# Where the sums of the exponentials come from: ScalarE's accumulator in one batch, a column of ones in three

## The chip, the cores and the metric

The kernel runs on one core of a Trainium2 chip. A core has TensorE (PE, matrix products), VectorE (DVE), ScalarE (ACT), GpSimd (POOL) and SyncE (SP, which here only issues DMAs); they run side by side and wait for each other by semaphores. The metric is the device time of the core in microseconds, the median of several executions.

## What is computed

Four batches of 12800 rows of 128 floats go through two attention steps against 32 inducing points, then through a gated product with a short causal convolution in the gate:

```python
def mab(q, kv):
    s = scale * (q @ kv.transpose(0, 2, 1))
    s = s - s.max(-1, keepdims=True)
    a = np.exp(s)
    a /= a.sum(-1, keepdims=True) + 1e-09
    return a @ kv
h = mab(I, x)                       # I: 32 inducing points, x: (4, 12800, 128)
x = mab(x, h)
...
for k in range(5):
    gate_pre += conv_w[k][None, None, :] * xp[:, k:k + S, :]
gate = 1.0 / (1.0 + np.exp(-gate_pre))
val = x @ w_val
return gate * val @ w_out
```

## The kernel before

**Tiling.** The 12800 rows of a batch are four strips of 3200, and a batch is cut into seven chunks of 320 to 480 columns per strip (`SIZES`). Each chunk of x comes twice: transposed, with channels on the partitions (`xt`, always a DMA), and with rows on the partitions (`xk`). For all chunks of batch 0 but one, `xk` is made on the chip by transposes on PE (`tp`, L289) and copies out of PSUM (`tpev`, L295 on ACT or L297 on DVE); for the others it is a second DMA (L258).

**The first attention of a batch.** `s1` (L315) multiplies a chunk by the inducing points, `e1` (L320, DVE) scales it into `ss` and takes the maximum; a group of chunks gets one maximum (`gm`, L337, `ng`, L365 and L367, on POOL or DVE), and then every chunk an exponential on ACT (`x1`, L375), a 32x32 transpose on DVE (`tr`, L379) and the product with `xk` on PE (`h`, L393). The products are summed in `H` (`ha`, L405 to L409). A later group has another maximum, so that what was summed before is scaled by `f` (L345).

**The sums of the exponentials.** They come from ACT: L375 has `accum_out`, which leaves the sum over a chunk's columns in a column of `zc`. Each such instruction is followed in the trace by an ACTIVATION_READ_ACCUMULATOR. When a new group comes, POOL scales the earlier columns of `zc` by `f` (`zs`, L355); at the end DVE adds the columns to `zt` (L360), PE brings `zt` into the layout of the result (`hz`, L428), and DVE takes the reciprocal (`zz`, L436 and L437). In parallel PE brings `H` into that layout (`hh`, L428), and DVE multiplies the two (`hT`, L440). `hT` is the 32x128 result h, transposed.

**What hangs on hT.** The weights of the later products (`w2`, `W`, `wo`) are derived from it (L447 to L541), and the second attention starts from it: `s2` (L555), `tin`, `mx` on DVE, `sub` (L574, POOL), `ex` (L580, ACT), `sm` (L586 to L591, DVE), `nm` (L597, POOL), `tout` (L600, DVE), and the halves of the probabilities in 16 bits, `phi` (L603, ACT) and `plo` (L605, POOL).

**The gated product.** `visit` (L622 gates, L629 values) is the convolution and the value product of a chunk on PE; `th` (L720, ACT), `gv` (L730, DVE), `hi` (L737, ACT) and `lo` (L740, POOL) make its 16-bit halves; `o` (L811, PE) is the last product, `ev` (L823 on DVE, L825 on ACT) the copy out of PSUM, `st` (L829) the store. The very last half chunk has its own path (L766 to L782).

**Order.** Nothing is scheduled at run time or by a planner: `ORDER` lists the operations one by one, each engine gets its own in this order, `SLOTS` gives every tile its buffer and `ENGINES` the engine where two can do an operation. Each engine works through its list in order, so an instruction that waits holds up all behind it. Loads of all kinds and the stores share one queue on SP.

## Time and profile before

| | us |
|---|---|
| median of 3 runs | 268.63 (267.71 to 269.29) |
| the profiled execution | 267.8 |
| its span, first to last instruction | 266.0 |
| PE busy | 260.3 (98%) |
| DVE busy | 220.4 (83%) |
| POOL busy | 202.4 (76%) |
| ACT busy | 192.4 (72%) |

The span lies 1.8 us below the time of the same execution; the rest is outside of what the instructions cover. The engines' busy times add up to far more than the span because they overlap. A PE that is busy throughout is not a PE at its peak: its matmuls overlap each other in the record. Mean time per instruction, what ended the idle time of an engine, and the chain of work that ended last say more than the shares.

### The profile page before, as it was taken

The numbers are of one execution on the slowest core, as the hardware profiler recorded it, in microseconds if no ns is written. First come the engines' busy times: TensorE is split into PE (matmuls) and PEld (weight loads), VectorE is DVE, ScalarE is ACT, GpSimd is POOL, SyncE is SP. The second block draws the span as 40 slices with busy tenths as digits, with TensorE's granted clock in tenths as the row PEclk, the third lists the DMA queues.
The fourth block names the chain that finished last, engine by engine and source line by source line (L and its number), as shares of the span: only waits on it lengthen the run. The fifth ranks groups of instructions, "written<-read, shape, count | busy, mean of one in ns | idle before, by whom it ended". The sixth has DMA issues, their size and how long they took to land.

```text
span 266.0 us, 10388 instructions
## 1 busy us (share of the span) xinstructions
PE 260.3 (98%) x4480; PEld 143.1 (54%) x4480; DVE 220.4 (83%) x438; ACT 192.4 (72%) x266; POOL 202.4 (76%) x182
## 2 busy tenths in 40 slices
PE   8999989999999999999999999999999999999994
PEld 4668343764544446584454456567545554444442
DVE  0789999997989999876998999896899897875534
ACT  2168249699759688687868599876689788787862
POOL 1013367999969878699897959999989989889660
PEclk9999999999999999999999999999999999999999
DMA  7999999699986699979998799884350324254476
GB/s 255 429 412 417 418 417 386 211 394 400 385 313 277 223 307 340 392 269 333 329 328 327 280 328 327 305 282 181 117 209 4 140 94 187 113 191 167 151 284 246
DMA packets 23229, 74.28 MB, mean 279 GB/s; under 512 B 1936, under 2 KB 16272, under 8 KB 23184
## 3 DMA queue, kind: packets, MB, share of 16 engines
q1 hardware_dynamic: 22896, 73.43, 73.5%
q8 instruction: 35, 0.57, 0.9%
q10 hardware_dynamic: 288, 0.20, 0.2%
q14 instruction: 10, 0.08, 0.1%
HBM read 47.40 MB, written 26.21 MB: 277 GB/s over the span
## 4 chain that ended last, share of the span: by engine, by line
PE 90%; DVE 8%; ACT 1%; issue 1%; POOL 0%; DVEq 0%; POOLq 0%
PE banks L622 33%; PE banks L811 24%; PE banks L555 7%; PE banks L393 7%; PE banks L315 7%; PE banks L629 6%; PE banks L289 2%; DVE et L379 2%; PE banks L216 1%; DVE ss L320 1%; PE banks L766 1%; PE banks L506 1%; DVE ng L367 1%; DVE e L559 0%; DVE z L586 0%
## 5 line engine op out<-in xcount | busy, mean ns | idle before, releaser
L740 POOL TENSOR_TENSOR gl<-tg,gh 128x960 f16<-128x960 f32 (+2 forms) x54 | 104.3, 1945 | 10.4 <-PE banks L811 5.2
L622 PE MATMUL banks<-P,W 32*128 32x480 f16 (+3 forms) x1680 | 103.9, 351 | 0.7 <-ACT P L603 0.7
L730 DVE SCALAR_TENSOR_TENSOR tg<-tg,banks 128x960 f32<-128x960 f32 (+4 forms) x57 | 61.2, 1078 | 21.7 <-ACT tg L720 14.1
L622 PEld LDWEIGHTS <-W 32*128 32x128 f16 x1680 | 51.4, 92 | 45.7 <-issue 14.9
L720 ACT ACTIVATE tg<-banks,gsc 128x960 f32<-128x960 f32 (+4 forms) x57 | 54.9, 1005 | 20.2 <-PE banks L622 18.1
L811 PE MATMUL banks<-gh,wo 128*32 128x448 f16 (+5 forms) x558 | 63.5, 358 | 0.0
L737 ACT CAST gh<-tg 128x960 f16<-128x960 f32 (+2 forms) x54 | 51.3, 961 | 11.0 <-DVE tg L730 8.7
L811 PEld LDWEIGHTS <-wo 128*32 128x32 f16 (+1 forms) x837 | 36.4, 97 | 32.8 <-issue 11.0
L811 PE MATMUL banks<-gl,wo 128*32 128x448 f16 (+4 forms) x279 | 43.5, 357 | 0.0
L629 PE MATMUL banks<-P,W 32*128 32x480 f16 (+3 forms) x336 | 41.3, 353 | 0.0
L825 ACT ACTIVATE os<-banks,osc 128x960 f32<-128x960 f32 (+2 forms) x30 | 30.5, 1024 | 6.3 <-PE banks L811 6.0
L597 POOL TENSOR_TENSOR e<-e,z 128x960 f32<-128x960 f32 (+4 forms) x17 | 24.9, 1467 | 6.2 <-DVE z L589 2.9
L393 PE MATMUL banks<-xk,et 128*32 128x128 f32 x800 | 29.5, 274 | 0.0
L823 DVE TENSOR_SCALAR os<-banks,osc 128x960 f32<-128x960 f32 (+1 forms) x24 | 27.9, 1168 | 1.4 <-PE banks L811 1.4
L605 POOL TENSOR_TENSOR P<-pt,P 128x960 f16<-128x960 f32 (+4 forms) x17 | 27.8, 1637 | 1.2 <-ACT P L603 0.9
L393 PEld LDWEIGHTS banks<-xk,et 128*32 128x32 f32 x800 | 24.8, 110 | 5.3 <-issue 1.5
L574 POOL TENSOR_TENSOR e<-e,m 128x960 f32<-128x960 f32 (+4 forms) x17 | 24.9, 1465 | 2.4 <-DVE m L569 2.4
L315 PE MATMUL banks<-xt,indT 128*32 128x480 f32 (+2 forms) x208 | 25.1, 556 | 0.0
L555 PE MATMUL banks<-xt,hT 128*32 128x480 f32 (+2 forms) x208 | 24.7, 557 | 0.0
L603 ACT CAST P<-pt 128x960 f16<-128x960 f32 (+4 forms) x17 | 14.0, 825 | 9.0 <-DVE pt L600 6.2
L559 DVE STREAM_TRANSPOSE e<-banks 128x480 f32<-128x480 f32 (+2 forms) x28 | 18.1, 652 | 1.7 <-PE banks L555 1.4
L375 ACT ACTIVATE ss<-ss,ng 128x480 f32<-128x480 f32 (+3 forms) x28 | 18.6, 665 | 0.6 <-POOL ng L367 0.6
(107 smaller groups left out, 269.8 us busy)
## 6 DMA issues: line engine op xcount, KB each, us to landing
out_dram<-os SPq DMA_DIRECT2D x30, 480.0 KB, 4.4
xt<-in_xt_dram SPq DMA_DIRECT2D x14, 960.0 KB, 8.9
xk<-in_xk_dram SPq DMA_DIRECT2D x11, 896.0 KB, 9.7
out_dram<-os SPq DMA_DIRECT2D x22, 448.0 KB, 4.5
xk<-in_xk_dram SPq DMA_DIRECT2D x10, 960.0 KB, 8.7
xt<-in_xt_dram SPq DMA_DIRECT2D x8, 896.0 KB, 11.0
xt<-in_xt_dram SPq DMA_DIRECT2D x3, 512.0 KB, 5.2
xt<-in_xt_dram SPq DMA_DIRECT2D x3, 448.0 KB, 5.9
```

The lines of the kernel that those rows point to most:

```text
L315: T.matmul(buf(key)[32 * r:32 * r + 32, :n], c_["indT"], x[:, :, r, :], start=True, stop=True)
L393: T.matmul(buf(key)[32 * s:32 * s + 32, :P], buf(("et", b, c))[:, 32 * i:32 * i + 32], buf(("xk", b, c))[:, i, :], start=j < R, stop=j >= ...
L555: T.matmul(buf(key)[32 * r:32 * r + 32, :n], buf(("hT", b)), x[:, :, r, :], start=True, stop=True)
L622: T.matmul(buf(("ps2", "g", b, c, r // 2))[:, r % 2, :n], buf(("W", b))[q, w, k, :], c_[("P1", "P2")[e]][q, o:o + n], start=u == 0, stop=u ...
L629: T.matmul(buf(("ps2", "v", b, c, r // 2))[:, r % 2, :n], buf(("W", b))[q, w, TAPS, :], c_[("P1", "P2")[e]][q, o:o + n], start=u == 0, sto ...
L720: lambda s=s: S.activation(buf(tg)[:, s, :n], buf(g)[:, s, :n], AF.Tanh, scale=small[b]["gsc"]),
L730: V.scalar_tensor_tensor(t, t, 1.0, buf(v)[:, s, :n], ALU.add, ALU.mult)
L737: op(("hi", b, c, p), "ACT", lambda: S.copy(buf(g1)[:, :, :n], buf(tg)[:, :, :n]), ("act", 2 * n), [("gv", b, c, p, 0)], [g1], [tg])
L740: ENG[e].tensor_tensor(buf(g2)[:, :, :n], buf(tg)[:, :, :n], buf(g1)[:, :, :n], ALU.subtract)
L811: T.matmul(t[s], w[:, s], x, start=j == 0, stop=j == len(terms) - 1)
L823: V.tensor_scalar(o, a, small[b]["osc"], None, ALU.mult)
L825: S.activation(o, a, AF.Copy, scale=small[b]["osc"])
```

## The change

Only batch 0 (`ACC = {0}`) keeps the sums from ACT's accumulator. In batches 1 to 3:

- each block of 128 channels in `xk` gets a 129th column that holds 1.0. The host writes it into the array that is loaded; a row of a load grows from 15 x 128 to 15 x 129 floats and is rounded up to a multiple of 16 (1920 to 1936 floats, 1792 to 1808). The tiles `xk` and `H` are as wide in all batches, the copies of batch 0 write 128 of every 129.
- the matmuls of `h` stream 129 columns instead of 128, so that the 129th column of `H` is the sum of the exponentials, and the scaling by `f` that `H` gets anyway covers it. `ha` works on 129 columns.
- `x1` has no `accum_out`; `zs`, `zt`, `hz` and `zz` are no operations of their own any more (3 of each). `hh` makes both products, one with the 128 columns of `H` and one with its last column, and `hT` does the reciprocal and the product one behind the other.

`ORDER`, `SLOTS` and `ENGINES` are new throughout. PE's list has 35 runs of `visit` pieces between other work in both versions.

```diff
+ACC = {0}
 def row(n):
-    return n // 32 * P
+    return -(-n // 32 * (P + 1) // (16 * PARTS * TRANSFERS)) * 16 * PARTS * TRANSFERS
...
-        op(("ones", b, c), "POOL", lambda: None, 0.001, pieces(b, c, [0]), [key])
+        if b in ACC:
+            op(("ones", b, c), "POOL", lambda: None, 0.001, pieces(b, c, [0]), [key])
+        else:
+            op(("ones", b, c), "POOL", lambda: G.memset(buf(key)[:, :n, P:], 1.0), 0.13, pieces(b, c, [0]), [key])
...
-                dst = buf(key)[:, g:g + k]
+                dst = buf(key)[:, g:g + k, :P]
...
         for c in cs:
             exp1(b, g, c)
+        if b not in ACC:
+            return
...
-            S.activation(e, e, AF.Exp, bias=small[b]["ng"][:, g:g + 1], scale=SCALE,
-                         accum_out=small[b]["zc"][:, turn(b, c):turn(b, c) + 1])
+            kw = dict(accum_out=small[b]["zc"][:, turn(b, c):turn(b, c) + 1]) if b in ACC else {}
+            S.activation(e, e, AF.Exp, bias=small[b]["ng"][:, g:g + 1], scale=SCALE, **kw)
...
+        w = P if b in ACC else P + 1
...
-                        T.matmul(buf(key)[32 * s:32 * s + 32, :P], buf(("et", b, c))[:, 32 * i:32 * i + 32],
-                                 buf(("xk", b, c))[:, i, :], start=j < R, stop=j >= len(parts) - R)
+                        T.matmul(buf(key)[32 * s:32 * s + 32, :w], buf(("et", b, c))[:, 32 * i:32 * i + 32],
+                                 buf(("xk", b, c))[:, i, :w], start=j < R, stop=j >= len(parts) - R)
...
+        def f_h(form):
+            over(form, buf(key), buf(H)[:, :P])
+            over(form, buf(key)[:, M:], buf(H)[:, P:].broadcast_to([P, P]))
+        def f_zn():
+            f_z(buf(key)[:, M:2 * M])
+            f_n()
...
+        else:
+            op(("hh", b), "PE", f_h, 0.49, [last[b], "const"], [key], [H], "out", 0.2)
+            op(("hT", b), "DVE", f_zn, 0.79, [("hh", b)], [hT], [key])
...
 ORDER = [
-    0, 1, 15, 2, 13, 16, 17, 18, 19, 20, 21, 23, 22, 30, 29, 14, 3, 49, 32, 31, 133, 57, 134, 33, 34, 132, 35,
...
```

**Place 1: batch 0, the copies of the transposed x.** DVE's list from the first copy on, before (`xk`, `ss`, `mx`, `m`, `n` and `ng` as above, `banks` is PSUM):

```order
L297 COPY xk_113<-banks 128x896
L320 TENSOR_SCALAR ss_72,mx_129<-banks 128x480
L297 COPY xk_115<-banks 128x1024
L320 TENSOR_SCALAR ss_73,mx_129<-banks 128x480
L297 COPY xk_115<-banks 128x896
L337 TENSOR_REDUCE m_130<-mx_129 128x1
L297 COPY xk_116<-banks 128x1024
L320 TENSOR_SCALAR ss_74,mx_129<-banks 128x480
```

DVE's list at the same place in the changed kernel:

```order
L324 TENSOR_SCALAR ss_72,mx_129<-banks 128x480
L324 TENSOR_SCALAR ss_73,mx_129<-banks 128x480
L341 TENSOR_REDUCE m_130<-mx_129 128x1
L371 TENSOR_SCALAR n_131<-m_130 64x1
L373 TENSOR_SCALAR ng_132<-n_131 32x1 x4
L324 TENSOR_SCALAR ss_74,mx_129<-banks 128x480
```

ACT's list from its first copy on in the changed kernel (L299 is the copy, L382 is `x1`, L349 is `f`):

```order
L299 COPY xk_113<-banks 128x8x128
L299 COPY xk_113<-banks 128x7x128
L299 COPY xk_115<-banks 128x8x128
L382 ACTIVATE ss_72,zc_146<-ss_72,ng_132 128x480
L382 ACTIVATE ss_73,zc_146<-ss_73,ng_132 128x480
L299 COPY xk_115<-banks 128x7x128
L299 COPY xk_113<-banks 128x8x128
L349 ACTIVATE f_133<-ng_132 128x1
```

Of the twelve copies of batch 0, eleven are now ACT's (seven before), and the shifted maximum `ng` of the first and of the last group is DVE's instead of POOL's, that of the third group POOL's instead of DVE's. The flush of the weights (`w`, L198) goes from DVE to POOL, and the weights' load goes ahead of the load of batch 0's chunk 0 on SP.

**Place 2: batch 0, PE behind the result h.** PE's list from the first `s1` of batch 1 on (`hT` is read by `s2`, L555), before:

```order
L315 MATMUL banks<-xt_67,indT 32x448 x4
L555 MATMUL banks<-os,hT_111 32x352 x4
L468 MATMUL banks<-hT_111,w 32x32 x4
L555 MATMUL banks<-xt_62,hT_111 32x480 x4
L555 MATMUL banks<-xt_63,hT_111 32x480 x4
L315 MATMUL banks<-xt_68,indT 32x448 x4
L315 MATMUL banks<-xt_70,indT 32x448 x4
```

PE's list at the same place in the changed kernel (L319 is `s1`, L576 is `s2`, L489 the product of L468):

```order
L319 MATMUL banks<-xt_67,indT 32x448 x4
L576 MATMUL banks<-os,hT_111 32x352 x4
L576 MATMUL banks<-xt_62,hT_111 32x480 x4
L489 MATMUL banks<-hT_111,w 32x32 x4
L576 MATMUL banks<-xt_63,hT_111 32x480 x4
L319 MATMUL banks<-xt_68,indT 32x448 x4
L576 MATMUL banks<-xt_64,hT_111 32x480 x4
L319 MATMUL banks<-xt_69,indT 32x448 x4
```

Before, the weights' transposes follow, then one `s2`, one `s1` and one `s2`, and the first visit. Now they follow with one `s1` among them, and then the first visit: one `s2` of 480 columns has gone behind the start of the visits.

**Place 3: batch 1, the result h on DVE.** DVE's list from the sum of the accumulator's columns (L360) on, before:

```order
L360 TENSOR_REDUCE zt_166<-zc_165 128x1
L730 SCALAR_TENSOR_TENSOR tg_86<-tg_86,banks 128x960
L407 SCALAR_TENSOR_TENSOR H_95<-H_95,f_152,banks 128x128
L436 TENSOR_SCALAR zz_153<-banks 128x32
L437 RECIPROCAL zz_153<-zz_153 128x32
```

Thirteen rows further stands L440, the product of L437's reciprocal with `H`. DVE's list around that product in the changed kernel:

```order
L416 TENSOR_TENSOR H_95<-H_95,banks 128x129
L324 TENSOR_SCALAR ss_72,mx_167<-banks 128x448
L439 TENSOR_SCALAR zz_153<-banks 128x32
L440 RECIPROCAL zz_153<-zz_153 128x32
L443 TENSOR_TENSOR hT_112<-banks,zz_153 128x32
```

The reciprocal stood apart from the product and ahead of it; now it comes behind the last sum of `H`, directly ahead of the product.

## Rows read from the trace of the kernel before

**Rows 1.** The page's head and its first part: engine, busy us, share, instructions.

```profile
span 266.0 us, 10388 instructions
...
PE 260.3 (98%) x4480; PEld 143.1 (54%) x4480; DVE 220.4 (83%) x438; ACT 192.4 (72%) x266; POOL 202.4 (76%) x182
```

**Rows 2.** The chain that ended last, share of the span by engine.

```profile
PE 90%; DVE 8%; ACT 1%; issue 1%; POOL 0%; DVEq 0%; POOLq 0%
```

**Rows 3.** Busy us of each engine in stretches, the first behind batch 0's result.

```profile
26.60:33.25 6.65, 6.17 (x115) 2.64 (x111) 6.30 (x26) 1.41 (x4) 2.00 (x4) 1.00 1.02 418
33.25:39.90 6.65, 5.94 (x142) 3.21 (x138) 6.47 (x22) 3.10 (x6) 4.52 (x8) 1.00 1.01 417
39.90:46.55 6.65, 6.65 (x96) 2.39 (x98) 6.29 (x16) 6.57 (x14) 5.08 (x11) 1.00 0.93 385
252.70:259.35 6.65, 6.65 (x86) 3.23 (x78) 2.30 (x3) 4.44 (x5) 4.01 (x3) 1.00 0.77 284
```

**Rows 4.** PE in order of time: start, us, instructions, idle before.

```profile
21.72 0.75 PE L315 MATMUL banks<-os,indT 128*32 128x320 f32 x8
...
28.88 0.27 PE L428 MATMUL banks<-pick,H 128*32 128x32 f32 x8 [0.44 <-DVE H L407]
...
34.39 0.99 PE L555 MATMUL banks<-xt,hT 128*32 128x480 f32 x8
...
37.65 0.59 PE L622 MATMUL banks<-P,W 32*128 32x320 f16 x12 [0.71 <-ACT P L603]
```

**Rows 5.** Groups by shape: count, busy us, mean ns; accumulator reads, sums of their columns.

```profile
L375 ACT ACTIVATION_READ_ACCUMULATOR ss<-ss,ng 128x1 f32 x28 | 5.3, 188 | 0.0
...
L360 DVE TENSOR_REDUCE zt<-zc 128x1 f32<-128x7 f32 x4 | 0.5, 124 | 0.0
```

**Rows 6.** Groups by shape: copies out of PSUM on either engine.

```profile
L823 DVE TENSOR_SCALAR os<-banks,osc 128x960 f32<-128x960 f32 x12 | 14.3, 1202 | 0.7 <-PE banks L811 0.7
...
L295 ACT COPY xk<-banks 128x896 f32<-128x896 f32 x3 | 2.7, 903 | 6.1 <-PE banks L289 6.1
```

**Rows 7.** Groups by shape: the products h and hh, and the reciprocal.

```profile
L393 PE MATMUL banks<-xk,et 128*32 128x128 f32 x800 | 29.5, 274 | 0.0
...
L428 PE MATMUL banks<-pick,H 128*32 128x32 f32 x32 | 1.5, 197 | 0.4 <-DVE H L407 0.4
...
L437 DVE RECIPROCAL zz<-zz 128x32 f32<-128x32 f32 x4 | 1.4, 353 | 0.1
```

**Rows 8.** The page's DMA issues: KB each, median us from issue to landing.

```profile
xk<-in_xk_dram SPq DMA_DIRECT2D x10, 960.0 KB, 8.7
```

**Rows 9.** DVE in order of time, batch 0: start, us, instructions.

```profile
21.14 0.21 DVE L365 TENSOR_SCALAR n<-m 64x1 f32<-64x1 f32 x1
21.38 0.86 DVE L367 TENSOR_SCALAR ng<-n 32x1 f32<-32x1 f32 x4
...
22.53 0.49 DVE L320 TENSOR_SCALAR_CACHE_REDUCE ss<-banks 128x320 f32<-128x320 f32 x1
...
23.29 0.15 DVE L337 TENSOR_REDUCE m<-mx 128x1 f32<-128x7 f32 x1
...
26.71 0.50 DVE L379 STREAM_TRANSPOSE et<-ss 128x320 f32<-128x320 f32 x1
...
27.43 0.43 DVE L198 SCALAR_TENSOR_TENSOR w<-tg,tg 128x261 f32<-128x261 int32 x1
...
29.41 0.19 DVE L440 TENSOR_TENSOR hT<-banks,zz 128x32 f32<-128x32 f32 x1
```

**Rows 10.** POOL in order of time, batch 0.

```profile
24.09 1.35 POOL L367 TENSOR_SCALAR ng<-n 32x1 f32<-32x1 f32 x4
...
35.18 0.78 POOL L597 TENSOR_TENSOR e<-e,z 128x352 f32<-128x352 f32 x1 [0.64 <-ACT e L580]
```

**Rows 11.** ACT in order of time, batch 0.

```profile
25.68 0.55 ACT L375 ACTIVATE ss<-ss,ng 128x320 f32<-128x320 f32 x1
...
37.11 0.49 ACT L603 CAST P<-pt 128x352 f16<-128x352 f32 x1 [0.55 <-DVE pt L600]
```

More of the change, by code (lines that the diff above doesn't have):

```diff
@@ L120, in tile_kernel @@
     wide = [tile_of(f"xk{i}", [P, row(32 * XB)]) for i in range(BUFS["xk"])]
-    store["xk"] = [t.rearrange("p (i c) -> p i c", c=P) for t in wide]
+    store["xk"] = [t[:, :XB * (P + 1)].rearrange("p (i c) -> p i c", c=P + 1) for t in wide]
     osall = tile_of("os", [P, BUFS["os"], 2, CW])
@@ L374, in f @@
             e = buf(ss)[:, :n]
-            S.activation(e, e, AF.Exp, bias=small[b]["ng"][:, g:g + 1], scale=SCALE,
-                         accum_out=small[b]["zc"][:, turn(b, c):turn(b, c) + 1])
-        op(("x1", b, c), "ACT", f, ("act", n, 0.29), [("ng", b, g)], [], [ss])
+            kw = dict(accum_out=small[b]["zc"][:, turn(b, c):turn(b, c) + 1]) if b in ACC else {}
+            S.activation(e, e, AF.Exp, bias=small[b]["ng"][:, g:g + 1], scale=SCALE, **kw)
+        op(("x1", b, c), "ACT", f, ("act", n, 0.29 if b in ACC else 0.1), [("ng", b, g)], [], [ss])
         op(("tr", b, c), "DVE", lambda: V.transpose(buf(et)[:, :n], buf(ss)[:, :n]), ("dve", n), [("x1", b, c)], [et], [ss])
@@ L402, in acc @@
         def acc():
-            t = buf(key)[:, :P]
+            t, a = buf(key)[:, :w], buf(H)[:, :w]
             if first:
-                V.tensor_copy(buf(H), t)
+                V.tensor_copy(a, t)
             elif scaled:
-                V.scalar_tensor_tensor(buf(H), buf(H), small[b]["f"][:, g:g + 1], t, ALU.mult, ALU.add)
+                V.scalar_tensor_tensor(a, a, small[b]["f"][:, g:g + 1], t, ALU.mult, ALU.add)
             else:
-                V.tensor_tensor(buf(H), buf(H), t, ALU.add)
+                V.tensor_tensor(a, a, t, ALU.add)
         last[b] = op(("ha", b, cs[0]), "DVE", acc, 0.285,
@@ L420, in prep @@
         sm = small[b]
-        key, zkey, H = ("ps", "hT", b), ("ps", "hz", b), ("H", b)
+        key, H = ("ps", "hT", b), ("H", b)
+        hT = ("hT", b)
         def over(form, t, x):
@@ L428, in over, with f_z, f_n @@
                 T.matmul(t[q, :M], x[:, q], c_["pick"], start=True, stop=True)
-        op(("hz", b), "PE", lambda form: over(form, buf(zkey), sm["zt"].broadcast_to([P, P])), 0.26, [("zt", b), "const"], [zkey], [],
-           "out", 0.2)
-        op(("hh", b), "PE", lambda form: over(form, buf(key), buf(H)), 0.26, [last[b], "const"], [key], [H], "out", 0.2)
-        hT = ("hT", b)
-        def f_z():
-            V.tensor_scalar(sm["zz"], buf(zkey)[:, :M], EPS, None, ALU.add)
-            V.reciprocal(sm["zz"], sm["zz"])
-        op(("zz", b), "DVE", f_z, 0.55, [("hz", b)], [], [zkey])
-        op(("hT", b), "DVE", lambda: V.tensor_tensor(buf(hT), buf(key)[:, :M], sm["zz"], ALU.mult), 0.25, [("hh", b), ("zz", b)],
-           [hT], [key])
+        def f_z(t):
+            V.tensor_scalar(sm["zz"], t, EPS, None, ALU.add)
+            V.reciprocal(sm["zz"], sm["zz"])
+        def f_n():
+            V.tensor_tensor(buf(hT), buf(key)[:, :M], sm["zz"], ALU.mult)
+        def f_h(form):
[4 more added lines that the diff above has]
+            f_n()
+        if b in ACC:
+            zkey = ("ps", "hz", b)
+            op(("hz", b), "PE", lambda form: over(form, buf(zkey), sm["zt"].broadcast_to([P, P])), 0.26, [("zt", b), "const"],
+               [zkey], [], "out", 0.2)
+            op(("hh", b), "PE", lambda form: over(form, buf(key), buf(H)[:, :P]), 0.26, [last[b], "const"], [key], [H], "out", 0.2)
+            op(("zz", b), "DVE", lambda: f_z(buf(zkey)[:, :M]), 0.55, [("hz", b)], [], [zkey])
+            op(("hT", b), "DVE", f_n, 0.25, [("hh", b), ("zz", b)], [hT], [key])
+        else:
+            op(("hh", b), "PE", f_h, 0.49, [last[b], "const"], [key], [H], "out", 0.2)
+            op(("hT", b), "DVE", f_zn, 0.79, [("hh", b)], [hT], [key])
         w2, wf, W = ("w2", b), ("wf", b), ("W", b)
@@ L1030 @@
             o += n
-    xn = x.reshape(B, R, NB, 32, C).transpose(0, 1, 3, 2, 4).reshape(B, R * 32, NB * C)
+    xn = _np.ones((B, R, 32, NB, C + 1), x.dtype)
+    xn[..., :C] = x.reshape(B, R, NB, 32, C).transpose(0, 1, 3, 2, 4)
+    xn = xn.reshape(B, R * 32, NB * (C + 1))
     xk = _np.zeros((B, P * max(sum(map(row, s)) for s in SIZES)), x.dtype)
     for b in range(B):
-        at = 0
+        o = at = 0
         for n in SIZES[b]:
-            xk[b, P * at:P * (at + row(n))] = parted(xn[b, :, at:at + row(n)])
-            at += row(n)
+            v = _np.zeros((P, row(n)), x.dtype)
+            m = n // 32 * (C + 1)
+            v[:, :m] = xn[b, :, o:o + m]
+            xk[b, P * at:P * (at + row(n))] = parted(v)
+            o, at = o + m, at + row(n)
     def bits(a):
```

6 lines of the change are left out of this document (3 added, 3 removed), and 160 rows, old and new, of tables (ENGINES, ORDER, SLOTS).

## The prediction

> **What bounds the kernel.** I read the engines' totals first [rows 1]: PE is busy for 260.3 of 266.0 us, DVE for 220.4, POOL 202.4, ACT 192.4. A busy PE need not be a full one, so the chain comes next [rows 2]: 90% of what ended last is PE, 8% DVE. Then the stretches [rows 3]: in all 33 stretches of 6.65 us from 39.90 to 259.35 (the first and the last of them stand there) PE is busy for the whole 6.65, while each other engine has free time in most. Only between 26.60 and 39.90, behind the result h of batch 0, is PE short of work after it has begun: 6.17 and 5.94 of 6.65. The two waits are in the list in order of time [rows 4]: 0.44 us ahead of `hh` for DVE's last sum, 0.71 us ahead of the first visit for `phi`, together 1.15 us. So from the first visit (37.65) on the time is PE's work, and ahead of it a chain through DVE, ACT and POOL that ends in that visit. A change pays by taking PE work away, by an earlier first visit, or by removing waits that the overlap of PE's records hides; it costs by the reverse. Time saved on ACT as such is worth nothing.
>
> **Part 1, the accumulator.** 21 of 28 accumulator reads go: 21 x 0.188 = 3.95 us of ACT [rows 5]. Three sums on DVE go, 3 x 0.124 [rows 5], and three short scalings on POOL. None is on PE's path from 39.90 on, so directly 0. It is spent in the new order: ACT takes four more copies of batch 0 and three more copies to `os`. A copy of 896 columns is 0.90 us on ACT, one of 960 columns 1.20 on DVE [rows 6]. With smaller pieces moved beside these, DVE loses about 9 us in all and ACT gains about 4, so that ACT ends near 196 and DVE near 211.
>
> **Part 2, the 129th column.** The 28 products `h` take 29.5 us of PE for 800 matmuls [rows 7]; the 600 of batches 1 to 3 are 22.1 us. One column in 128 more is 0.17 us. Before has no odd width; the widths that it has are multiples of 32, and the next such width would be 160, 25% or 5.5 us more. I take 0.17, since the matmuls of 128 columns and more in the trace cost by the column, and keep 0 and 5.5 as ends. Less than 0 is excluded: no column goes.
>
> The products `hz` go and come back inside `hh`: an `hh` is 1.5 / 4 = 0.37 us [rows 7], an `hz` is of the same kind, and their number stays, so 0 on PE. But they and the reciprocal now stand between the last sum of `H` and `hT`: 0.37 of PE and about 0.55 of DVE (0.35 is the reciprocal [rows 7], the rest the instruction ahead of it and the step between), 0.9 us in each of three batches. What covers it: behind `hh` PE has a whole visit ahead of the first `s2` in batches 1 and 2, and two products `o` in batch 3. DVE, which now waits in front of the reciprocal, holds back a `gv` or a transpose; the tanh ahead of that `gv` is out by then. I take 0; with the cover gone it would be 0.9 once, in batch 3.
>
> **Part 3, longer rows of loads.** 21 loads of `xk` grow by 0.8%. A load of 960 KB takes 8.7 us from issue to landing [rows 8], but at 418 GB/s [rows 3] it is 2.35 us of transfer; the rest is queue. 0.8% is 0.02 us each, 0.4 us in all, and it falls on loads issued ahead of need: 0, with 0.4 as the other end.
>
> **Part 4, the start.** PE's list up to `s1` of chunk 0 holds the same work as before in another order, and the weights' load ahead of that chunk's costs 0.26 MB at 418 GB/s = 0.6 us of landing, on a chunk used only at 21.7 [rows 4]. So DVE's `e1` of that chunk stays at 22.53 [rows 9]; with its 0.49 us and the maximum (0.15 us at 23.29 [rows 9]) the last `ng` can begin at 23.4. Before, POOL ended it at 24.09 + 1.35 = 25.44 [rows 10]; on DVE it takes 0.21 + 0.86 = 1.1 [rows 9] and ends at 24.5. On ACT, the third group's `ng` is POOL's now and some 0.6 slower, and a copy of 0.9 [rows 6] stands ahead of `f`, so that `x1` of chunk 0 starts at 25.2 against 25.68 [rows 11]. DVE's transpose follows at 26.6 (before 26.71 [rows 9]); from there to `hT` were 2.7 us, in which stood the flush of the weights (0.43 us, L198 [rows 9]), now POOL's, and a smaller piece of their conversion, by estimate 0.2, now earlier. `hT` starts at 28.65 instead of 29.41 [rows 9]: 0.75 us.
>
> From `hT` to the first visit: `sub` still waits for POOL to finish the low half of the weights, but `tin`, `mx` and `sm` of the first chunks now go ahead of two `e1` and one `g3l` on DVE. `nm` could start about 0.7 us sooner than 35.18 [rows 10], and `phi` follows it (37.11 before [rows 11]). The first visit would start at 37.65 - 0.75 - 0.7 = 36.2.
>
> Against that, one `s2` of 480 columns is now done behind it; its row has 0.99 us [rows 4], of which, since neighbours on PE overlap, I take 0.8 as an estimate. Net -0.65. The ends: 0, if PE or a load holds the chain, and -1.45, if the `s2` fills a wait. The whole 1.15 us of idle [rows 4] lies between.
>
> **Behind the first visit** the list is nearly the same: 35 runs of visits in both, the same products between. Waits that the overlap of PE's records hides don't show in busy times, and a `lo` on POOL ahead of a product `o` or a load ahead of an `h` can come late in any new order. For an emptier DVE I take -0.2; the ends are -1.5 (as much again as the start can give) and +1.0 (about one DVE instruction of the size of those in [rows 6] coming late once).
>
> **The sum:** 0 + 0.17 + 0 - 0.65 - 0.2 = -0.7 us, from 267.8 to 267.1 for the profiled execution. The median of the runs lies 0.3% above that execution, so 268.63 x 267.1 / 267.8 = **267.9 us**. About 0.5% (1.3 us) is what a measurement can tell from no change, so this is "the same".
>
> **Rivals.**
>
> *The whole gain arrives.* DVE is at 6.3 of 6.65 in both stretches behind batch 0 and in the next [rows 3]; if its 9 us are what PE's hidden waits hang on, the 1.45 us stay and another 1.0 comes: -1.45 - 1.0 + 0.17 = -2.3, so 266.3. For it: ACT waits little there. Against it: the recorded waits of PE are only 1.15.
>
> *The start is moved, not shortened.* ACT's eleven copies stand ahead of its exponentials, each 0.9 us; if one group waits for one, `hT` is where it was, and the visits are no earlier. Only the 0.17 is left: 268.8.
>
> *The odd pitch costs PE* (the other side). Each block of `xk` starts 516 bytes behind the one before, and PE, the bound, reads it in all 300 blocks. At the full step to the next width it is 5.5 us, at half of it 2.75: 267.9 + 2.6 = 270.5. It decides from 2.2 us on, 10% on `h`. For it: no row of before has an odd width or pitch. Against it: PE reads a chunk for `s1` in pieces of 32 with steps between, at the rate by the column.
>
> The Trainium skill speaks against the change here: "SBUF — State Buffer", section "Door 1: The DMA port swizzle", says that SBUF is read in lines of 16 bytes and that each crossing to a new line costs. 128 floats off such a boundary touch 33 lines instead of 32; as an estimate by that page that is 3% of the matmuls' time, 0.7 us instead of 0.17, and 268.4 instead of 267.9 for the whole, short of the point at which this rival decides. No run so far shows it.
>
> **Chances.** Forecast 0.40, whole gain 0.30, moved 0.15, odd pitch 0.15. A fifth of the forecast's own spread lies below -0.5%. So faster 0.30 + 0.08 = 0.38, same 0.32 + 0.15 = 0.47, slower 0.15. The range takes in the whole gain with some tenths to spare, 265.8, and upward the late product (+1.0) and the beginning of the odd pitch, 270.1; the most of the odd pitch is left out.
>
> **What would show it.** The first visit at 36.2 and `hT` at 28.65 (part 4); seven accumulator reads, ACT near 196 and DVE near 211 us (part 1); the mean of an `h` matmul at 276 ns against 274, above 300 for the odd pitch (part 2); PE busy for 6.65 in all stretches from 39.90 on, with no idle behind `hh`. The forecast is wrong if the first visit is not earlier, or if it is and PE loses the time again behind it.

## The result, and the profile after

| | before | changed |
|---|---|---|
| median | 267.76 us (267.48 to 269.29, 6 runs) | 270.85 us (269.63 to 272.43, 6 runs) |
| ratio | | 1.0103, 95% interval 1.0061 to 1.0144 |
| the profiled execution | 267.8 | 270.0 |
| its span | 266.0 | 268.2 |

The forecast was 267.9 us with a range up to 270.1, and "slower" had a chance of 0.15. It was worked out from the median of three runs, 268.63, so as a ratio it said 0.997; the six runs of the table have a median of 267.76. The kernel is 1.0% slower. Measured again beside other kernels it gave 270.57 us, 1.0105 (1.0087 to 1.0124).

The page's head and its totals, the share of the chain of work by engine, and the seven accumulator reads that are left, to be held against [rows 1], [rows 2] and [rows 5]:

```profile
span 268.2 us, 10276 instructions
...
PE 260.0 (97%) x4438; PEld 140.0 (52%) x4438; DVE 213.2 (79%) x424; ACT 196.7 (73%) x254; POOL 203.4 (76%) x182
...
PE 82%; DVE 5%; DMA 4%; POOL 3%; ACT 3%; issue 1%; POOLq 0%; DVEq 0%; ACTq 0%
```

```profile
L382 ACT ACTIVATION_READ_ACCUMULATOR ss<-ss,ng 128x1 f32 x7 | 1.3, 188 | 0.0
```

PE is as busy as before (260.0 against 260.3) in a span that is 2.2 us longer, and its share of the chain fell from 90% to 82%: DMA, POOL and ACT, which had 1% or nothing there, have 10% together. So PE did not get more work; it waits. Busy us of each engine in stretches, as in [rows 3]:

```profile
26.60:33.25 6.65, 6.20 (x124) 3.07 (x117) 5.40 (x20) 1.55 (x4) 1.95 (x4) 1.00 1.02 417
33.25:39.90 6.65, 5.88 (x142) 3.03 (x137) 6.46 (x23) 3.59 (x8) 4.44 (x7) 1.00 1.01 418
39.90:46.55 6.65, 5.91 (x98) 2.27 (x94) 6.51 (x15) 5.85 (x10) 4.82 (x9) 1.00 0.96 392
73.15:79.80 6.65, 6.49 (x112) 2.62 (x104) 5.05 (x13) 5.00 (x7) 5.76 (x6) 1.00 1.06 393
179.55:186.20 6.65, 6.25 (x178) 4.92 (x174) 2.81 (x9) 5.50 (x7) 5.30 (x4) 1.00 0.35 129
```

Before, PE (the first number behind the comma) was busy for all of 6.65 in every stretch from 39.90 to 259.35. Now 39.90, 73.15, 179.55 and one at 53.20 are short of it. What PE waited for, in us, how often, and the longest:

```profile
PE banks L576 <- ACT tg L741: 0.7, 1, 0.7
PE banks L293 <- DMA xt<-in_xt_dram: 0.6, 1, 0.6
PE banks L400 <- DMA xk<-in_xk_dram: 0.4, 1, 0.4
PE banks L319 <- DVE ss L324: 0.4, 1, 0.4
PE banks L436 <- DVE H L414: 0.4, 1, 0.4
PE banks L643 <- ACT P L624: 0.4, 1, 0.4
PE banks L400 <- DVE et L385: 0.4, 1, 0.4
PE banks L643 <- POOL P L626: 0.2, 1, 0.2
PE banks L643 <- DVE e L580: 0.2, 1, 0.2
```

Four of them are new behind the first visit: an `s2` that waits for the tanh (0.7), an `h` that waits for a load of `xk` (0.4), and two visits that wait for `plo` (0.2) and for `tin` (0.2).

**A measure for where PE loses time.** Idle time in the record is too short by what overlaps. So I took the start of each piece of PE's work and subtracted the work that stands ahead of it in PE's list, each product priced at the pace of stretches without waits (0.80 us for an `s2` or `h` of 480 columns, 0.60 for a product `o`). The rest is PE's lag: warm-up, changes between kinds of products, and waits. It compares different orders, since it grows only where time is lost. In us at the start of some visits, for the kernel before (B), the changed one (C) and the experiments that follow (single executions):

```
visit (batch, chunk)    B      e9     e5     e1    e13     e7     C     e14    e15
first visit (0,0)     11.20  10.53  10.62  10.67  10.72  10.97  11.22  10.96  11.37
(1,1)                 17.70  17.03  17.02  17.11  17.18  19.00  19.25  18.85  19.23
(1,2)                 19.05  18.38  18.29  18.41  18.54  20.17  20.40  20.00  20.37
(1,3)                 19.42  18.75  19.10  19.23  19.36  20.98  20.77  20.37  20.74
(2,2)                 22.60  21.94  22.29  22.43  22.56  24.18  23.93  23.53  23.90
(2,3)                 23.38  22.80  23.65  23.82  23.45  25.56  25.43  25.17  24.65
end                   28.60  27.99  28.84  29.01  28.64  30.75  30.74  30.48  29.97
```

From C's first visit to (1,1) the lag grows by 8.03, in B by 6.50: 1.5 us. From (2,2) to (2,3) it grows by 1.50 against 0.78: 0.7 us. These two are the 2.1 us by which the end is later than in B (2.2 together, of which 0.1 comes back elsewhere).

### The profile page after: what moved, and what is told of

The parts are those of the page before. It is cut to its first block, busy times and chain, and to the rows that moved or that the text cites. A ratio compares the mean times of both kernels' runs of the same rounds, so it can differ in the third digit from the quotient of the medians.

```text
span 268.2 us, 10276 instructions
## 1 busy us (share of the span) xinstructions
PE 260.0 (97%) x4438; PEld 140.0 (52%) x4438; DVE 213.2 (79%) x424; ACT 196.7 (73%) x254; POOL 203.4 (76%) x182
## 2 busy tenths in 40 slices
DMA packets 23229, 74.46 MB, mean 278 GB/s; under 512 B 1936, under 2 KB 16272, under 8 KB 23184
## 4 chain that ended last, share of the span: by engine, by line
PE 82%; DVE 5%; DMA 4%; POOL 3%; ACT 3%; issue 1%; POOLq 0%; DVEq 0%; ACTq 0%
PE banks L643 29%; PE banks L832 23%; PE banks L319 8%; PE banks L576 7%; PE banks L400 5%; PE banks L650 5%; DMA xk<-in_xk_dram 3%; PE banks L293 3%; DMA xt<-in_xt_dram 1%; DVE ss L324 1%; POOL ng L373 1%; PE banks L787 1%; PE banks L527 1%; DVE tg L751 1%; POOL P L626 1%
## 5 line engine op out<-in xcount | busy, mean ns | idle before, releaser
L832 PE MATMUL banks<-gh,wo 128*32 128x448 f16 (+4 forms) x522 | 62.3, 358 | 0.0
L832 PEld LDWEIGHTS <-wo 128*32 128x32 f16 (+1 forms) x783 | 34.1, 97 | 33.6 <-issue 11.3
L832 PE MATMUL banks<-gl,wo 128*32 128x448 f16 (+5 forms) x261 | 42.4, 357 | 0.0
L846 ACT ACTIVATE os<-banks,osc 128x960 f32<-128x960 f32 (+2 forms) x32 | 32.7, 1030 | 8.6 <-PE banks L832 7.3
L844 DVE TENSOR_SCALAR os<-banks,osc 128x960 f32<-128x960 f32 (+2 forms) x22 | 25.4, 1164 | 5.8 <-PE banks L832 3.5
L400 PE MATMUL banks<-xk,et 128*32 128x129 f32 (+1 forms) x800 | 28.0, 274 | 0.8 <-DMA xk<-in_xk_dram 0.4
L319 PE MATMUL banks<-xt,indT 128*32 128x480 f32 (+2 forms) x208 | 25.8, 556 | 0.5 <-DVE ss L324 0.4
L576 PE MATMUL banks<-xt,hT 128*32 128x480 f32 (+2 forms) x208 | 24.3, 557 | 0.7 <-ACT tg L741 0.7
L324 DVE TENSOR_SCALAR_CACHE_REDUCE ss<-banks 128x480 f32<-128x480 f32 (+3 forms) x28 | 17.2, 621 | 9.3 <-PE banks L319 9.2
L382 ACT ACTIVATE ss<-ss,ng 128x480 f32<-128x480 f32 (+3 forms) x28 | 17.4, 665 | 5.2 <-POOL ng L373 3.1
```

Of the source, the lines that this page charges most:

```text
L319: T.matmul(buf(key)[32 * r:32 * r + 32, :n], c_["indT"], x[:, :, r, :], start=True, stop=True)
L400: T.matmul(buf(key)[32 * s:32 * s + 32, :w], buf(("et", b, c))[:, 32 * i:32 * i + 32], buf(("xk", b, c))[:, i, :w], start=j < R, stop=j >= ...
L576: T.matmul(buf(key)[32 * r:32 * r + 32, :n], buf(("hT", b)), x[:, :, r, :], start=True, stop=True)
L832: T.matmul(t[s], w[:, s], x, start=j == 0, stop=j == len(terms) - 1)
L846: S.activation(o, a, AF.Copy, scale=small[b]["osc"])
```

## The experiments

**Two theories.** Theory 1: the new *order* makes the kernel slower, by waits that the old one hadn't. Theory 2: the new *form* of the sums does it, be it by its width or by what hangs on it. The forms and the orders can be crossed, since both orders name the same operations.

**e1, the new form in the old order.**

```diff
 changed kernel, but
-ORDER, SLOTS, ENGINES of the changed kernel
+ORDER, SLOTS, ENGINES of the kernel before, without zs, zt, hz, zz of batches 1 to 3
```

> The column of ones in batches 1 to 3 as in the changed kernel (wider rows of xk, 129 columns in h, no accumulator, hh with two products), but the order, the buffers and the engines of the kernel before, with the removed operations left out of it. Theory 1, the new order makes the change slower (its 1.0%): then the form costs only the 0.17 us of the wider h and stands at 267.3 to 268.5 us, ratio to the kernel before 0.998 to 1.003. Theory 2, the form makes it slower (odd pitch, longer rows of loads, the reciprocal behind the last sum of H): then 269.5 to 271 us, ratio 1.007 to 1.013.

268.58 us (268.40 to 269.01), ratio 1.0049 (1.0036 to 1.0063): between the two. In this run the order of all else is the old one, so that the steps of PE can be set side by side. Up to 117 us they agree within 0.07 us. Then two are longer. In batch 3 `s2` waits for `hT` (PE, then DVE, in order of time):

```profile
184.54 1.82 PE L576 MATMUL banks<-xt,hT 128*32 128x480 f32 x16 [0.38 <-DVE hT L443]
```

```profile
183.68 0.19 DVE L439 TENSOR_SCALAR zz<-banks 128x32 f32<-128x32 f32 x1 [0.85 <-PE banks L436]
183.91 0.35 DVE L440 RECIPROCAL zz<-zz 128x32 f32<-128x32 f32 x1
184.29 0.19 DVE L443 TENSOR_TENSOR hT<-banks,zz 128x32 f32<-128x32 f32 x1
```

In the kernel before DVE did the reciprocal five microseconds ahead, and only the last product behind `hh`:

```profile
178.13 0.18 DVE L436 TENSOR_SCALAR zz<-banks 128x32 f32<-128x32 f32 x1
178.35 0.35 DVE L437 RECIPROCAL zz<-zz 128x32 f32<-128x32 f32 x1
...
183.82 0.19 DVE L440 TENSOR_TENSOR hT<-banks,zz 128x32 f32<-128x32 f32 x1 [0.80 <-PE banks L428]
```

That step of PE (the product `o` ahead of `s2`) is 0.54 us longer than before. In batch 2 the `s2` has cover, as forecast, but the visit behind `hh` doesn't: two of its pieces are 0.27 and 0.16 us longer. Its second piece writes gates into the PSUM bank that holds the result of `hh`, and that bank is free when `hT` has read it, now 0.6 us later. Together 0.97 us, against 1.3 us (1.0 to 1.7) by the ratio. In batch 1 nothing is lost.

**e5, only the late reciprocal.**

```diff
 kernel before, batches 1 to 3:
-hz (zt into the layout), zz (reciprocal) as operations of their own, ahead
+hh: both products, the second from zt;  hT: reciprocal, then product
```

> The kernel before, with its accumulators, its 128 columns, its pitch and its loads; only hz and zz of batches 1 to 3 are moved: hh makes both products, the second from zt, and hT does the reciprocal ahead of its product, as in the changed kernel. Theory A, the reciprocal behind the last sum of H is what the form costs: in the run with the old order and the column, PE waits 0.54 us for hT ahead of the first s2 of batch 3 and 0.43 us in the visit behind hh of batch 2, so 0.8 to 1.3 us, ratio to the kernel before 1.003 to 1.005. Theory B, the 129 columns, the odd pitch or the longer loads cost it: no difference, ratio 0.999 to 1.001.

268.58 us (267.84 to 268.93), ratio 1.0030 (1.0017 to 1.0043): theory A. With accumulators, 128 columns and the old loads, the moved reciprocal alone costs 0.8 us, and the lag grows at the same two places (column e5).

**e9, only the wide rows.**

```diff
 changed kernel in the order of the kernel before
-ACC = {0}
+ACC = {0, 1, 2, 3}
```

> The kernel before with its order and its accumulators in all batches; only the layout is that of the changed kernel: each block of xk 129 floats wide, rows of loads up to 1936 floats, tiles of xk and H one column wider. h streams 128 columns. Theory A (the late reciprocal is what the form costs): no difference, ratio 0.999 to 1.001. Rival (the odd pitch or the longer loads cost PE something): 1.002 or more, 268.0 us and above; the pure pitch rival of the forecast would show it in the mean of h, 274 ns in the kernel before.

267.37 us, ratio 1.0007 (0.9995 to 1.0019): no difference. The group of `h`, count, busy us, mean ns; first this kernel with 128 columns out of rows of 129, then the changed one with 129:

```profile
L400 PE MATMUL banks<-xk,et 128*32 128x128 f32 x800 | 29.5, 273 | 0.2
```

```profile
L400 PE MATMUL banks<-xk,et 128*32 128x129 f32 x600 | 21.2, 274 | 0.4 <-DMA xk<-in_xk_dram 0.4
```

So the odd pitch and the longer loads cost nothing that can be measured: 0.2 us by the ratio (-0.1 to 0.5). This kernel still computes 128 columns; the price of the 129th shows only in the second line's mean, 274 against 273.

**e13, the wait for hT taken out of e1.** In batch 3 the last load, and so the last `h`, is chunk 4's, but its sum comes first in the group, with two more sums behind it.

```diff
 as e1, but
-GROUPS of batch 3 = [[0, 1, 2, 3], [4, 5, 6]];  DVE: sums of chunks 4, 5, 6
+GROUPS of batch 3 = [[0, 1, 2, 3], [5, 6, 4]];  DVE: sums of chunks 5, 6, 4
-PE: o(2,1,2), o(2,1,3), hh(3), o(2,0,1), s2(3,1)
+PE: o(2,1,2), hh(3), o(2,1,3), o(2,0,1), s2(3,1)
```

> The run with the old order and the column of ones (ratio 1.005), but in batch 3 the sums of H of the second group go in the order 5, 6, 4 instead of 4, 5, 6, so that only one sum stands behind the last product h, and hh goes ahead of the last product o but one. hT is then done about 0.5 us earlier against the s2 that waited 0.54 us for it. If the wait for the late reciprocal is what that run loses in batch 3: 0.4 to 0.6 us back, 267.9 to 268.2, ratio 1.0025 to 1.0035, with no wait of PE for hT in the trace. If the time is given back at once (hh then waits for the sums): 268.5, ratio 1.0045 to 1.0055.

268.14 us (267.30 to 268.42), ratio 1.0016 (1.0005 to 1.0028). Of e1's 0.49%, 0.33 points are back, or 0.9 us, give or take 0.5 by the two intervals; by the lag table it is 0.37 us (29.01 to 28.64 at the end). PE no longer waits for `hT`:

```profile
183.63 0.56 PE L832 MATMUL banks<-gh,wo 128*32 128x448 f16 x8
184.01 0.37 PE L832 MATMUL banks<-gl,wo 128*32 128x448 f16 x4
184.20 1.80 PE L576 MATMUL banks<-xt,hT 128*32 128x480 f32 x16
```

What is left, 0.16% or 0.43 us, is of the size of the wait for the bank in batch 2. So in the old order the form costs the late reciprocal, and nothing else that these runs can tell from 0.2%.

**e2, the old source of the sums in the new order.**

```diff
 changed kernel, but
-x1 without accum_out in batches 1 to 3, h with 129 columns, hh from H's last column
+x1 with accum_out, zs and zt back, h with 128 columns, hh's second product from zt
```

> The order, buffers and engines of the changed kernel, but the sums of all batches come from ScalarE's accumulator: h has 128 columns, the scalings of zc and the sums zt are back in batches 1 to 3, and hh takes its second product from zt instead of the column of H. Loads and pitch stay as in the changed kernel. Theory 1, the new order: no better than the changed kernel, 270.5 to 272 us, since 21 accumulator reads of 0.19 us and three short operations come on top; ratio to the kernel before 1.009 to 1.016. Theory 2, the form: 267.5 to 268.5 us, as far as it is the width of h or the wait behind H; ratio 0.998 to 1.004.

270.61 us (269.80 to 271.13), ratio 1.0119 (1.0102 to 1.0137): theory 1. In the new order it makes no difference that these runs can tell whether ScalarE's accumulator or the column gives the sums.

**e10, the new order with the reciprocal early.** As e2, with `hz` ahead of the last `h` and `zz` right behind the last sum of `H`.

> As the run with the new order and the accumulators (270.6 us, ratio 1.012), but hz ahead of the last products h and zz right behind the last sum of H, so that the reciprocal is done while PE makes hh, as in the kernel before. If the late reciprocal costs as much in the new order as in the old one (0.8 us): 269.8, ratio 1.008 to 1.010. If the new order covers it (two products o behind hh in batch 3) and its waits are others: 270.4 to 270.8, ratio 1.011 to 1.0135.

271.92 us, ratio 1.0174 (1.0158 to 1.0190): slower than both expectations. `hz` needs a bank of PSUM of its own, and where it stands all banks are taken. Three waits are new:

```profile
PE banks L400 <- DVE tg L751: 0.9, 1, 0.9
...
PE banks L832 <- DVE tg L751: 0.4, 1, 0.4
...
PE banks L436 <- ACT tg L741: 0.3, 1, 0.3
```

So this run does not tell what the late reciprocal costs in the new order. It does show that the old form can't be put back into this order for free: the bank that the new form saves has been used.

**e7, e6, e8 and e12, the orders joined.** A piece of one order up to a visit, then the rest of the other (PSUM banks and buffers of the second part exchanged so that they fit).

```diff
 changed kernel, ORDER, SLOTS, ENGINES
+e7:  new up to visit (1,1), then old      e8:  old up to visit (1,1), then new
+e6:  new up to visit (0,0), then old      e12: old up to visit (0,0), then new
```

> The column of ones; the new order up to the first piece of the visit of batch 1, chunk 1 (about 105 us), the old one behind it. At that visit PE's lag behind its own work is 1.55 us larger in the changed kernel than in the kernel before. If that is the new order's share there, and the reciprocal costs about 1.0 us in the old order of batches 2 and 3 behind it: 269.6 to 270.0, ratio 1.009 to 1.0105. If the waits of the new order hang on one another, so that a later part gives back what an earlier one lost: 268.4 to 269, ratio 1.004 to 1.0065.

270.79 us (270.01 to 271.02), ratio 1.0111 (1.0094 to 1.0128), as slow as the new order throughout. Its lag at (1,1) is 1.9 us above e1's, and behind it grows like e1's (11.75 to the end against 11.90). So what the order costs against e1 (1.0049) comes before 107 us.

> The column of ones; the order, buffers and engines of the changed kernel up to the first visit, those of the kernel before behind it. The forecast of the start (-0.65 us) against the run with the old order throughout (268.6): 267.9, ratio to the kernel before 1.0025. If the start is only moved (the s2 that is left behind takes the 0.8 us that the first visit comes earlier): 268.4 to 268.8, ratio 1.004 to 1.006.

270.01 us, ratio 1.0087 (1.0072 to 1.0102). Slower than either expectation, and not clean: at the joint an `s2` waits 1.1 us for the bank that the copy of `W` frees.

```profile
PE banks L576 <- ACT W L536: 1.1, 1, 1.1
```

It does show a reason to put this `s2` (chunk 4) behind the first visit: with the banks as they are given here, none was free in time ahead of it.

> The column of ones; the old order up to the same visit, the new one behind it. PE's lag grows by another 0.6 us in the changed kernel behind that visit, and the new order has two products o between hh of batch 3 and the s2 that waits for hT. If the lags add: 267.7 to 268.1, ratio 1.002 to 1.0035, which is less than the old order throughout. If the second part is bound by something that does not move with PE (loads of xk, POOL), it loses more when it begins earlier: 268.8 to 269.8, ratio 1.006 to 1.010.

> The column of ones; the order, buffers and engines of the kernel before up to the first visit, those of the changed kernel behind it. In the trace of the changed kernel PE loses 1.3 us more than before between the first visit and 107 us, of which 0.76 in one s2 that waits for a bank of PSUM. If that loss hangs on the s2 of chunk 4 that the new start leaves behind the first visit, it is gone here: 269.2 us, ratio 1.005 to 1.007. If it lies in the order behind the first visit whatever the start: 270.3 to 270.9, ratio 1.010 to 1.013.

276.53 us (1.0328) and 275.83 us (1.0313). Neither time tells what a half costs: the second part expects loads that the first part hadn't issued, and at the joint PE waits once for 5.6 us (`xk`, e8) and once for 4.5 us (`xt`, e12). In e12 the clock adds to it: behind that wait, from 43 to 46 us, the mean granted clock (behind the counts) is 0.54, where it was 1.00 ahead of it, and the `s1` there takes 1.72 us, where the one at 34.64 took 0.96.

```profile
43.00:46.00 3.00, 2.27 (x16) 0.52 (x20) 0.00 (x0) 0.00 (x0) 0.51 (x1) 0.54 0.95 398
```

One thing e12 does tell. It has the old start, so the `s2` of chunk 4 stands ahead of the first visit (36.98 us), and the `s2` of chunk 5 still waits for the tanh, as long as in the changed kernel:

```profile
35.39 1.02 PE L576 MATMUL banks<-xt,hT 128*32 128x480 f32 x8
36.98 2.22 PE L643 MATMUL banks<-P,W 32*128 32x320 f16 x58 [0.57 <-ACT P L624]
...
51.55 1.01 PE L576 MATMUL banks<-xt,hT 128*32 128x480 f32 x8 [0.74 <-ACT tg L741]
```

**e4, ng of the third group back on DVE.**

```diff
 changed kernel, ENGINES
-ng(0,2): POOL
+ng(0,2): DVE
```

> The changed kernel with ng of batch 0's third group on DVE, as in the kernel before, instead of POOL. In the trace of the changed kernel POOL takes from 20.81 to 23.14 us for it, and f on ACT waits 0.56 us for it. If that wait is what kept hT where it was, x1 of chunk 0 comes 0.5 us earlier and hh starts at 28.4 instead of 28.87, time 270.4. If DVE is what bounds the start, its 1.1 us push e1 of chunk 0 and the last ng back by about 1 us, and hh starts at 29.0 to 29.9, time 271 to 271.9.

270.90 us (270.29 to 271.91), ratio 1.0137 (1.0114 to 1.0161). The start gets worse, as under the second expectation: `e1` of chunk 0 goes to 24.34 us (22.91 in the changed kernel), PE then waits 1.5 us for a transpose, and the first visit begins at 38.07.

```profile
PE banks L400 <- DVE et L385: 1.5, 1, 1.5
```

The time hardly follows: of 1.2 us that the first visit is later, 0.4 are left at the end. The wait for `xk` at 182 us is gone in this run, since PE comes later than the load.

**e3, the late h.** In the changed kernel `xk` of batch 3's chunk 4 can be loaded when `h` of chunk 2 has freed its buffer. PE, in order of time:

```profile
182.12 0.97 PE L400 MATMUL banks<-xk,et 128*32 128x129 f32 x27 [0.40 <-DMA xk<-in_xk_dram]
```

```diff
 PE, changed kernel
-h(3,6), o(2,0,2), h(3,4), o(2,0,0), o(2,0,1)
+h(3,6), o(2,0,2), o(2,0,0), h(3,4), o(2,0,1)
```

> The changed kernel with one product h (batch 3, chunk 4) behind the next product o instead of ahead of it. In the trace it waits 0.76 us for a load of xk that lands at 181.98 us. If PE's waits for such loads are what the new order costs, 0.5 to 0.8 us come back: 270.1 to 270.4 us against 270.9. If the lost time is given back later (hh of batch 3 and the s2 behind it come later by the same), the time stays at 270.9 and the lag of PE at the visits behind 188 us is as in the changed kernel.

270.37 us (269.61 to 270.82), ratio 1.0107 (1.0088 to 1.0126). No clear gain, and in the trace the lag between (2,2) and (2,3) grows by 1.48, as in the changed kernel: the product `o` now in front begins 0.3 us late, and `hh` and the `o` before it take the rest. The wait was moved.

**e11, the changed kernel again.**

> The changed kernel as it is, beside the others of this call. 270.4 to 271.0 us, ratio 1.0105 to 1.013, if the three runs with the new order and the column so far (270.4 to 270.9) are one level; that the first measurement of 270.85 was a slow chip would show as 268 to 269.

270.57 us (269.43 to 271.30), ratio 1.0105 (1.0087 to 1.0124). One level.

**e14, a gv ahead of the reciprocal.**

```diff
 DVE, changed kernel, batch 1
-e1(2,2), hT(1) with its reciprocal, gv(0,3,1)
+e1(2,2), gv(0,3,1), hT(1) with its reciprocal
```

> The changed kernel with one move on DVE: in batch 1, gv of chunk 3's second half goes ahead of hT with its reciprocal instead of behind it. The chain that ends in the visit at 78 us (hT 0.73 us, gv, the cast, the tanh, the next gv, the transpose that frees the bank) then begins 0.45 us earlier. If the late reciprocal costs the new order the waits of 0.34 and 0.17 us there: 0.4 to 0.5 us back, 270.1 to 270.4, ratio 1.0085 to 1.0100. If a later wait (xk of batch 3's chunk 4 at 182 us) takes it up, as it did in the run with the late h: 270.5 to 270.9, ratio 1.0105 to 1.0125, with PE's lag at 90 us 0.4 us smaller and at 190 us the same.

270.12 us (269.85 to 270.39), ratio 1.0102 (1.0085 to 1.0119). The wait of the visit at 78 us for `tin` is gone, and the wait for `xk` at 182 us is 0.2 us longer in its place: 0.15 us won by the visits behind 81 us, and lost again at the load. From the first visit to the end the lag grows by 19.52, as in the changed kernel; what column e14 has less than C throughout, 0.26 us, is an earlier start of this execution. The second expectation.

**e15, the cause of the late load removed as well.**

```diff
 as e14, and
-PE: o(1,6,1), o(1,6,2), o(1,6,3), h(3,2), h(3,3);  SP: st(1,6,0), xk(3,4)
+PE: o(1,6,1), h(3,2), o(1,6,2), o(1,6,3), h(3,3);  SP: xk(3,4), st(1,6,0)
```

> The changed kernel with the move of the run before (gv ahead of hT in batch 1) and a second one: h of batch 3's chunk 2 goes two products o earlier (1.2 us), and the load of xk for chunk 4, whose buffer that h frees, goes directly behind it, ahead of a store. In the changed kernel this load is issued at 173.94 us, lands at 181.98, and h of chunk 4 waits 0.76 us for it. If these two waits are what the new order loses and nothing takes their place: 1.1 us back, 269.4 to 269.8, ratio 1.006 to 1.008. If the next link (the products o that wait for POOL's lo, or hh) takes it up, as with the late h: 270.1 to 270.6, ratio 1.0095 to 1.0115, with no wait for xk in the trace.

269.79 us (269.25 to 271.67), ratio 1.0066 (1.0043 to 1.0089). The first expectation: about 1.0 us of the 2.8 that the changed kernel loses in the same measure (1.0105) is back by two moves, though the two intervals just touch. There is no wait for `xk` in the trace, the lag between (2,2) and (2,3) grows by 0.75 as in the kernel before, and from the first visit to the end it grows by 18.60 against 19.52: 0.92 us less.

## Why the prediction was wrong, and where it was right

The forecast of 267.9 was below by 3 us, and the range's upper end by 0.75. The rival on the slower side came near the time (270.5) by luck: its mechanism is excluded. Two steps failed: the start, and the term for what comes behind the first visit. Measured as the prediction's sum, between the two profiled executions the width is 0.2, the start 0 in place of -0.65 and the rest +2.1 in place of -0.2, together about the 2.2 us between the spans.

**What bounds the kernel: right, and it pointed at the result.** The time is PE's work behind the first visit, and ACT's saved time was worth nothing: 21 reads went, and ACT was busy for 196.7 us in all (196 forecast), DVE for 213.2 (211). The lesson that I drew too weakly is the reverse: when PE has no spare time, every new wait counts in full, and the old order had almost none to give back.

**Part 2, the width: small, as forecast.** 0.17 us was taken; that is too little for these runs to confirm. The mean of `h` is 274 ns at 129 columns, and the sign of 276 did not show. The rival of the odd pitch is excluded: its own sign, above 300 ns, is absent. The Trainium skill, "SBUF — State Buffer", says in the section "Door 1: The DMA port swizzle" that SBUF is read in lines of 16 bytes, that two accesses in a row to the same line are enough for full bandwidth, and that each access that crosses to a new line pays a penalty. Rows of fp32 that are read in one piece meet that condition of two accesses, on or off a line's start, and the trace agrees with it: 273 ns with the odd pitch, 274 without. The 0.7 us that the prediction worked out from the crossings did not come (e9: -0.1 to 0.5 us).

**Part 2, the late reciprocal: wrong in the old order, and nearly right in the new one.** I priced it well (0.9 us a batch), named the right instructions, and then took 0, "with the cover gone 0.9 once, in batch 3". In the old order it costs 0.54 us in batch 3 (e1, undone in e13) and 0.43 in batch 2, the second by a path that I had not looked at: I asked who waits for `hT`'s *value*, and not who waits for the PSUM *bank* that `hT` reads. In the new order, which the prediction was about, batches 2 and 3 pay next to nothing: from (1,2) to (1,3) the lag grows by 0.37 in C as in B, from (2,2) to (2,3) by 0.75 in e15 against 0.78 in B, where two products `o` stand behind `hh` of batch 3. In batch 1 the `gv` that DVE holds back in front of the reciprocal cost 0.15 us (e14). So this step is a small part of the miss.

**Part 4, the start: wrong by its terms.** Forecast was `hT` at 28.65 and the first visit at 36.2, net -0.65 us. POOL, ACT and DVE in the changed kernel, to be held against [rows 9 to 11]:

```profile
20.81 0.38 POOL L371 TENSOR_SCALAR n<-m 64x1 f32<-64x1 f32 x1 [3.64 <-DVE m L341]
21.28 1.86 POOL L373 TENSOR_SCALAR ng<-n 32x1 f32<-32x1 f32 x4
```

```profile
23.18 0.29 ACT L349 ACTIVATE f<-ng 128x1 f32<-128x1 f32 x1 [0.56 <-POOL ng L373]
...
25.71 0.55 ACT L382 ACTIVATE ss<-ss,ng 128x320 f32<-128x320 f32 x1
```

```profile
29.41 0.19 DVE L443 TENSOR_TENSOR hT<-banks,zz 128x32 f32<-128x32 f32 x1
```

```profile
28.87 0.27 PE L436 MATMUL banks<-pick,H 128*32 128x32 f32 x8 [0.39 <-DVE H L414]
...
36.87 2.24 PE L643 MATMUL banks<-P,W 32*128 32x320 f16 x58 [0.38 <-ACT P L624]
```

`hT` is at 29.41, to the hundredth where it was, which is chance. The step that failed is the one from DVE's transpose of chunk 0 to `hT`. That transpose came at 26.68 (26.6 forecast, 26.71 before), and the flush and the other piece that were to make the 2.7 us behind it shorter were gone, as forecast. But it took 2.73 us again, since DVE now waits there for PE's products `h`:

```profile
24.84 1.24 DVE L385 STREAM_TRANSPOSE et<-ss 128x480 f32<-128x480 f32 x2
...
26.68 0.50 DVE L385 STREAM_TRANSPOSE et<-ss 128x320 f32<-128x320 f32 x1
...
27.57 0.35 DVE L414 SCALAR_TENSOR_TENSOR H<-H,f,banks 128x128 f32<-128x128 f32 x1 [0.35 <-PE banks L400]
28.47 0.35 DVE L414 SCALAR_TENSOR_TENSOR H<-H,f,banks 128x128 f32<-128x128 f32 x1 [0.56 <-PE banks L400]
```

PE at that place, in the changed kernel and before:

```profile
25.57 2.74 PE L400 MATMUL banks<-xk,et 128*32 128x128 f32 x78 [0.37 <-DVE et L385]
```

```profile
25.38 2.83 PE L393 MATMUL banks<-xk,et 128*32 128x128 f32 x80
```

Before, PE was at these products until 28.2 as well, and DVE did the flush meanwhile. So PE held the chain there, and taking the flush from DVE could give little: that is the prediction's own end of 0, "if PE or a load holds the chain". They also begin 0.2 us later now. DVE's two transposes for them stand behind the last `ng`, which is now DVE's, and the exponentials that they read are late: I let the third group's `ng` cost 0.6 us more on POOL; it took 2.33 us there (20.81 to 23.14) against 0.21 + 0.86 on DVE [rows 9], and the exponentials of two chunks, a copy and then chunk 0's exponential queue behind it on ACT (25.71, where 25.2 was forecast).

The first visit did come 0.78 us earlier than in this execution of the kernel before, and the `s2` of 0.8 us that was left behind takes all of it: lag 11.22 against 11.20. So the term came out as the rival "moved, not shortened" has it, by another cause: PE's own products, and not a copy ahead of an exponential. Over more executions it was a loss. The old kernel's profiled one began slowly: its first 15 transposes took PE 2.93 us, 2.04 in e9. In the six other runs with the old start `hT` is at 28.74 to 29.12 and the lag at the first visit 10.5 to 10.9; in eight with the new start and no edit to it, at 29.13 to 29.90 and 10.96 to 11.71, on average 0.6 us more. That fits the runs, which differ by 2.8 us by the ratio, while the two spans differ by 2.2. The new start also has less to spare on its loads: in e3, e6 and e11 an `s1` waits 0.5 to 0.7 us for one; with the old start the longest such wait ahead of the first visit is 0.2 (e12).

One reading behind the rival "the whole gain arrives" was wrong too. It had for it that ACT waits little in the two stretches behind batch 0; ACT is busy for only 1.41 and 3.10 of 6.65 there [rows 3]. That speaks against a gain from an emptier DVE alone.

**Behind the first visit: wrong in sign and in its end.** -0.2 was taken, with +1.0 as the end; it was +2.1. The places: `s2` of chunk 5 at 46.30, which waits for a bank that the tanh frees (0.76 us over the same place before); the visit at 55.8 for `plo` (0.22); visits at 78 and 81 us for DVE's transpose (0.34 and 0.17); `h` of batch 3's chunk 4 for its load (0.76). PE and ACT at the first:

```profile
46.30 1.01 PE L576 MATMUL banks<-xt,hT 128*32 128x480 f32 x8 [0.74 <-ACT tg L741]
```

```profile
45.19 2.01 ACT L741 ACTIVATE tg<-banks,gsc 128x960 f32<-128x960 f32 x2 [0.66 <-PE banks L643]
```

ACT waits for PE to finish the gates, and then PE waits for ACT to read them: a loop through a PSUM bank, which time freed on DVE did not shorten. All eight banks are in use there, and this `s2` gets the one whose gates ACT has yet to read. The `s2` that the start left behind is not the cause: in e12 it isn't there, and the wait is. So it belongs to the order behind the first visit. No order without this wait was tried, so what it is worth in time stays open. The load's wait and the one at 78 us are shown: e15 took out both, and by the lag table 0.75 us came back at the load and 0.17 ahead of (1,1). One alone gave nothing clear (e3, e14): e14's is taken up by the load's wait, and e3 moved the load's wait without undoing its cause.

"35 runs of visits in both, the same products between" was the evidence for a nearly equal rest. It was true and said nothing: what changed is which bank and which buffer each product gets and when it is free, and the list of PE does not show that.

**What stays open.** Of the changed kernel's 1.05%, e15 leaves 0.66%. By the traces that is the wait for the tanh and the start, some 0.8 and 0.6 us, and smaller ones; neither was undone alone, so their prices are read from the lag and not shown by a run. No version here beats the kernel before; the nearest with the new form is e13, 0.16% above it.

## What to carry over

When one engine's work fills the time, as PE's did here, freeing another engine won nothing, and each new wait counted: ask first what the new form puts *behind* the last input of the result (here a reciprocal behind the last sum), and price it at the wait of whoever needs the value and of whoever needs its bank. An order searched anew is a change of its own, and should be measured apart from the form: run the new form in the old order. For each product that moves, follow the buffer: who frees its PSUM bank or its load's buffer, and how much of the bound engine's work stands between the two. And before an instruction's time is subtracted from a chain, look for what runs beside it: here the bound engine's own products filled the same stretch.
